# The slot from which VectorE transposes h by way of DRAM: slot 7 in place of slot 12

## The chip, the cores and the metric

The kernel runs on one core of a Trainium2 chip. The time is device time in microseconds of that core, the median of the runs shown; the profile is one more execution, taken by the hardware profiler. TensorE (PE, its weight loads PEld), VectorE (DVE), ScalarE (ACT), GpSimd (POOL) and SyncE (SP) each work through a queue of their own, in order, and wait for one another by semaphores.

## The reference, cut to what matters

Attention with a block-causal mask (8 batches, 8 heads, 576 tokens, 64 wide), then a mixture of experts over its 4608 rows: each row goes to the one expert with the largest logit.

```python
expert_idx = np.argmax(logits, axis=1)
...
for e in range(E):                       # E = 8, D = 512, F = 1024
    mask = expert_idx == e
    ...
    h = np.maximum(x[mask] @ w1[e], 0.0)
    out[mask] = gate_w[mask, None] * (h @ w2[e])
```

All is computed in fp32. For a product the kernel splits each operand into a high part (rounded by a copy to fp32r) and a low part (what is left), and sums three products.

## The kernel before, in words

The first 440 us or so are the attention and the routing. The expert stage after it works in **slots** of 128 rows that belong to one expert; slots 1, 2, 3, ... are written out one after the other, and the order in which the code is written is the order on each engine. The first product of slot g (`layer1(g)`, lines 1046 and 1064) is 24 matmuls of 128x512 on TensorE into two halves `ph`, each turned into half of `h` by a ScalarE relu. The second (`layer2(g)`, lines 1046, 1093 and 1096) is 24 matmuls into `py`, scaled by ScalarE into `y` (`give`) and scattered to the output by GpSimd. `mm3` issues per chunk of 128 channels three matmuls: high part by high weight, high part by low weight, low part by high weight.

**Turning h.** The second product needs h with its channels on the partitions. Two ways are in the kernel.
- By TensorE (`ht`, line 1077): eight 128x128 transposes into `px`, then a ScalarE copy to `hh` and a VectorE subtraction to `hl` (lines 1085 and 1086).
- By VectorE: ScalarE's queue stores each half of h to DRAM as soon as its relu is done (`h_store`, line 1003); GpSimd's queue loads it back in another arrangement into `hq` (`h_load`, four DMAs, line 1011); VectorE transposes blocks of 32x32 into `px`, two instructions (`h_turn`, line 981); then the copy to `hh` and the subtraction to `hl`, each in two halves (`h_in`, lines 990 and 988).

There is one `hq`, one `hh` and one `hl`; `ph` and `px` have three buffers, `py` two. x is turned by VectorE in the same way from slot 7 on in both kernels (`x_turn`, then `xh` on ScalarE and `xl` on VectorE), gathered by GpSimd four slots ahead.

**Weights.** `raw[0]` and `raw[1]` hold the next expert's weights of the first and the second product in fp32. At the first slot of an expert they are split into the other half of `ring_h` (ScalarE, line 808) and `ring_l` (VectorE, line 812), in four pieces of 128x1024, two at a time, and SP then loads the expert after it into raw. At other slots the split is branched over.

What sets the order are the calls in `first` and `second`, which follow one another for each slot (`TURN` is 12, `LAG` is 10):

```python
def seconds(g):
    return g - 1 if g < LAG + 2 else g - 2
def first(g):
    ...
    if g <= LAG + 1:
        ht(g - 1)
    if g != LAG + 2:
        next_weights(seconds(g), 1, (0, 1))
    if g > 1:
        next_weights(g, 0, (2, 3))
    layer1(g, out=g < NU - 1)            # stores h where g >= TURN
def second(g):
    ...
    if g >= XTURN - 1 and g + 2 < NSLOT: # x_turn(g + 2), x_in, x_low
    ...
    if g != LAG + 2:
        next_weights(seconds(g), 1, (2, 3))
    ...
    next_weights(g + 1, 0, (0, 1))
    if g > TURN:
        h_turn(g - 1)
    if g >= TURN:
        h_load(g)
    if g <= LAG:
        layer2(g - 1)
    elif g > LAG + 1:
        layer2(g - 2, y=slots[g + 2]["xg"] if g + 2 < NSLOT else None)
    if LAG + 1 < g <= TURN:
        ht(g - 1)
    ...
    if g + AHEAD < NSLOT:
        fetch(g + AHEAD)
    if g > TURN:
        h_in(g - 1)
```

So with TURN at 12, slots 0 to 11 are turned by TensorE and slots from 12 on by VectorE; `second(11)` has no second product, and from `second(12)` on the second product runs two slots behind the first in place of one.

Of the kernel before, what the change touches and what calls it, by code (L numbers as in the profile page):

```python
# [34 lines left out]
def kernel(  # L35
# [879 lines left out]
        nc.vector.tensor_scalar(tab[:, 3, gs], eg[:, 0], float(E), None, op0=ALU.is_lt)  # L915

    AHEAD = 4
    TURN = 12
    LAG = TURN - 2
    XTURN = 6  # L920
    NFIRST = 4
# [21 lines left out]
    def next_weights(g, i, cs=range(NPC)):  # L943
        if g >= NSLOT:
            return
        sl = slots[g]
        if g == 0:
            for c in cs:
                split_hi(i, c, 1)
                split_lo(i, c, 1)  # L950
            load_raw(i, 2, cs)
            return
        body = sl["body", i]
        for en, fn in (("act", split_hi), ("dve", split_lo)):
            with tc.If(sl["to", en] != 0):  # L955
                to = sl["to", en] & 1
                for c in cs:
                    ins = fn(i, c, to)
                    for en2, c2, o in body:
                        if en2 != en and c2 != c:  # L960
                            tc.declare_no_dep(ins.ins, o.ins, reason="other columns of the ring")
                    body.append((en, c, ins))
        with tc.If(sl["first_sp"] != 0):
            load_raw(i, sl["en2"], cs)

    def fetch(g):
        slots[g]["xg"] = xg = take("xg")
        slots[g]["gate"] = take("gate")
        w = DM // GQ
        parts_of = [(xg, xbuf, rowi[:, g:g + 1])] if g <= XTURN else [  # L970
            (xg[:, j * w:(j + 1) * w], xunit, rowq[:, j, g:g + 1]) for j in range(GQ)]
        for to, src, at in parts_of + [(slots[g]["gate"], gbuf, rowi[:, g:g + 1])]:
            nc.gpsimd.indirect_dma_start(out=to, out_offset=None, in_=src,  # L973
                                         in_offset=bass.IndirectOffsetOnAxis(ap=at, axis=0))
# [27 lines left out]
    def h_store(g, f):  # L1002
        nc.scalar.dma_start(hrows[g % 2][f // 512], slots[g]["h"][:, f:f + 512])

    def h_load(g):

        slots[g]["hq"] = hq = take("hq")
        w = DF // GQ
        for q_ in range(GQ):
            rows = hrows[g % 2][q_ // 2]  # L1010
            nc.gpsimd.dma_start(hq[32 * q_:32 * q_ + 32].rearrange("j (g x) -> j g x", g=GQ),
                                rows[:, q_ % 2 * w:(q_ % 2 + 1) * w].rearrange("(g j) x -> j g x", g=GQ))

    def h_turn(g):
        slots[g]["ht"] = [turned(slots[g]["hq"], slice(f, f + 4), NF) for f in range(0, NF, 4)]

    def h_in(g, us=(0, 1)):
        if 0 in us:
            slots[g]["hT"] = take("hh"), take("hl")
        hh, hl = slots[g]["hT"]  # L1020
        for u in us:
            for w in range(2):
                part(w, hh[:, 4 * u:4 * u + 4], hl[:, 4 * u:4 * u + 4], slots[g]["ht"][u])
# [32 lines left out]
    def layer1(g, out=True):  # L1056
# [4 lines left out]
        for f in range(0, DF, 512):  # L1061
# [3 lines left out]
            slots[g]["h"] = h  # L1065
            if out and g >= TURN:
                h_store(g, f)

    def ht(g, fs=(0, 4), pts=None):
        for f in fs:  # L1070
            ht_copy(g, f, ht_pe(g, f, None if pts is None else pts[f // 4]))
# [28 lines left out]
    def layer2(g, cs=None, y=None):  # L1100
        if cs is None or 0 in cs:
            slots[g]["py"] = take("py")
        py = slots[g]["py"]
        mm3(g, 1, py, slots[g]["hT"], DM, NF, 0, cs)
        if cs is None or NF - 1 in cs:
            give(g, py, slots[g]["gate"][:, 0:1], outi[:, g:g + 1], y)
# [202 lines left out]
    def second(g):  # L1309
# [14 lines left out]
# [11 lines that stand above are left out]
# [5 lines left out]
# [4 lines that stand above are left out]
# [81 lines left out]
```

## Time and profile before

| | |
|---|---|
| median of three runs (lowest, highest) | 864.79 us (864.24, 872.6) |
| the profiled execution | 868.43 us, its span 866.7 us |
| PE busy in the span | 837.9 us (97%) |
| DVE, ACT, POOL busy | 581.5, 488.0, 595.3 us |
| mean granted clock of TensorE | 0.984 |
| bytes moved by DMA | 146.67 MB |

Busy time is time in which the engine had an instruction in work; idle time of an engine is laid to what released it. A granted clock of 1.00 is 2.4 GHz, one of 0.50 is 1.2 GHz.

### The profile page before, as it was taken

Reading aid. Unit: us, or ns where it says so; the run is one execution under the profiler, and the core shown is the slowest. Engines: PE = TensorE matmul, PEld = TensorE weight load, DVE = VectorE, ACT = ScalarE, POOL = GpSimd, SP = SyncE. Lnnn points to the kernel's source line nnn. Section 1 sums busy time; section 2 is a strip of 40 time slices with the busy share of each in tenths; the row PEclk is TensorE's granted clock in tenths of the full one; section 3 lists DMA queues with packets and bytes.
Section 4 is the critical chain, followed back from the end, with each engine's and each line's share of the span. In section 5 each row is a group of like instructions: output and inputs, shape, how many; then the busy total and the mean of one; then the engine's idle time right before and its main releaser. Section 6 shows DMA issues by size and latency. Waiting matters only on the chain. (4 is left out here: it accounts for less than half of the span.)

```text
span 866.7 us, 19006 instructions
## 1 busy us (share of the span) xinstructions
PE 837.9 (97%) x5148; PEld 677.5 (78%) x5148; DVE 581.5 (67%) x1275; ACT 488.0 (56%) x959; POOL 595.3 (69%) x756
## 2 busy tenths in 40 slices
PE   7989999999999999988899999999999999999996
PEld 4768887788877788856678888888888888888875
DVE  8648788888787888882976545745666544666441
ACT  4647776768686767765655534644645333553321
POOL 6555778788788787875644355556777877677872
PEclk9889999999999999998999999999999999999999
DMA  7967878888887889864538444556777554455441
GB/s 149 197 127 149 178 174 177 181 173 180 177 180 169 165 186 184 190 163 151 182 111 292 139 136 147 190 191 211 238 246 239 158 152 148 133 150 148 153 119 38
DMA packets 141531, 146.67 MB, mean 169 GB/s; under 512 B 98889, under 2 KB 108329, under 8 KB 139852
## 3 DMA queue, kind: packets, MB, share of 16 engines
q1 hardware_dynamic: 115868, 91.58, 44.0%
q0 software_dynamic: 18896, 41.45, 17.2%
q10 hardware_dynamic: 6624, 12.06, 3.9%
q8 instruction: 50, 0.82, 0.4%
q14 instruction: 93, 0.76, 0.3%
HBM read 85.12 MB, written 31.79 MB: 135 GB/s over the span
## 5 line engine op out<-in xcount | busy, mean ns | idle before, releaser
L367 DVE TENSOR_REDUCE nmx<-psm 128x1 f32<-128x320 f32 x315 | 134.7, 453 | 65.0 <-PE psm L365 60.4
L410 ACT ACTIVATE pT<-pss 128x448 f32<-128x448 f32 (+1 forms) x254 | 108.5, 449 | 51.6 <-PE pss L401 40.5
L391 POOL TENSOR_TENSOR pS<-pS,pT 128x320 f32<-128x320 f32 x189 | 112.4, 594 | 21.0 <-ACT pT L419 4.4
L401 PE MATMUL pss<-qx,kx 70*128 70x448 f32 (+1 forms) x382 | 109.4, 312 | 10.9 <-DMA qx<-nmT 10.9
L400 PE MATMUL pss<-qb,ka 128*128 128x448 f32 (+1 forms) x382 | 115.1, 313 | 0.3
L1046 PE MATMUL py<-ring_h,hh 128*128 (+1 forms) x288 | 112.7, 391 | 0.8 <-ACT h L1064 0.8
L1046 PE MATMUL py<-ring_h,hl 128*128 (+1 forms) x288 | 112.2, 390 | 0.0
L1046 PE MATMUL py<-ring_l,hh 128*128 (+1 forms) x288 | 112.1, 389 | 0.0
L391 POOL TENSOR_TENSOR pS<-pT 128x448 f32<-128x448 f32 x63 | 71.9, 1141 | 58.1 <-ACT pT L410 57.9
L1046 PE MATMUL ph<-ring_h,xh 128*128 x280 | 109.9, 393 | 0.0
L1046 PE MATMUL ph<-ring_h,xl 128*128 x280 | 109.3, 390 | 0.0
L1046 PE MATMUL ph<-ring_l,xh 128*128 x280 | 109.2, 390 | 0.0
L365 PE MATMUL psm<-kd,qd 128*128 128x320 f32 x315 | 106.2, 373 | 1.9 <-DVE idx L300 0.8
L435 PE MATMUL psb<-pT,vo 128*64 128x448 f32 (+4 forms) x768 | 96.5, 399 | 2.0 <-issue 1.0
L812 DVE TENSOR_TENSOR ring_l<-raw,ring_h 128x1024 f32 (+1 forms) x64 | 83.0, 1308 | 18.7 <-ACT ring_h L808 13.8
L1064 ACT ACTIVATE h<-ph 128x512 f32<-128x512 f32 x70 | 41.8, 598 | 79.4 <-PE ph L1046 68.0
L435 PEld LDWEIGHTS psb<-pT,vo 128*64 128x64 f32 x768 | 50.4, 138 | 45.1 <-issue 29.9
L401 PEld LDWEIGHTS pss<-qx,kx 70*128 70x128 f32 x382 | 73.8, 193 | 13.7 <-DMA qx<-nmT 7.3
L400 PEld LDWEIGHTS pss<-qb,ka 128*128 128x128 f32 x382 | 73.8, 193 | 7.4 <-ACT pT L410 3.4
L973 POOL DMA_INDIRECT xg<-xbuf,rowq x64 | 64.9, 1014 | 21.1 <-issue 18.6
L973 POOL DMA_INDIRECT ex<-xbuf,rowq x64 | 64.1, 1002 | 19.5 <-issue 15.8
L808 ACT CAST ring_h<-raw 128x1024 f32 (+1 forms) x68 | 70.3, 1053 | 6.5 <-ACTq L955 4.1
(278 smaller groups left out, 1812.3 us busy)
## 6 DMA issues: line engine op xcount, KB each, us to landing
raw<-in_moe_w_dram SPq DMA_DIRECT2D x40, 512.0 KB
ka<-kd SPq DMA_DIRECT2D x128, 144.0 KB
raw<-in_moe_w_dram SPq DMA_DIRECT2D x12, 1024.0 KB
hrows<-h ACTq DMA_DIRECT2D x46, 256.0 KB
hq<-hrows POOLq DMA_DIRECT2D x92, 128.0 KB
qn<-in_q_dram SPq DMA_DIRECT2D x64, 144.0 KB
kn<-in_k_dram SPq DMA_DIRECT2D x64, 144.0 KB
qx<-qb SPq DMA_DIRECT2D x32, 288.0 KB
```

What stands on the lines that cost most here:

```text
L365: nc.tensor.matmul(mx[:, 0:max(e - a, 256)], qd[d][:, j, :, :], kd[d][:, a:a + max(e - a, 256)], start=True, stop=True)
L367: nc.vector.tensor_reduce(m[:, j + u:j + u + 1], mx[:, 0:e - a], axis=AX.X, op=ALU.max, negate=True)
L391: eng.tensor_tensor(o, pT[0:r, P:S] if t == 1 else o, pT[0:r, off[t]:off[t] + w], op=ALU.add)
L400: nc.tensor.matmul(o, ka[i][:, hh, ts], qb[i][:, hh, c0:c1], start=True, stop=False)
L401: nc.tensor.matmul(o, kx[i][0:KX, hh, ts], qx[i][0:KX, hh, c0:c1], start=False, stop=True)
L410: nc.scalar.activation(pT[:, o:o + c1 - c0], st[:, 0:c1 - c0], AF.Exp, scale=scale)
L435: nc.tensor.matmul(ob[hh * D:(hh + 1) * D, c0:c1], a[:, t, hh, :], pTs[hh][0][:, o:o + c1 - c0], start=(t == 0), stop=(c0 == OB or t == NJ ...
L808: return nc.scalar.copy(piece(ring_h, to, c, half), raw[i][:, c * CW:(c + 1) * CW])
L812: return eng.tensor_tensor(piece(ring_l, to, c, half), raw[i][:, c * CW:(c + 1) * CW], piece(ring_h, to, c, half).bitcast(F32), op=ALU.sub ...
L973: nc.gpsimd.indirect_dma_start(out=to, out_offset=None, in_=src, in_offset=bass.IndirectOffsetOnAxis(ap=at, axis=0))
L1046: m = nc.tensor.matmul(out, a[:, c, :], w, start=(c == 0 and w is wh and a is sh), stop=(c == nk - 1 and a is sl_))
L1064: nc.scalar.activation(h[:, f:f + 512], ph, AF.Relu)
```

## The change

The number TURN goes from 12 to 7, and LAG with it from 10 to 5. Slots 7 to 11 are now turned by VectorE by way of DRAM; TensorE turns slots 0 to 6. `second(6)` has no second product (it was `second(11)`), and the two slots' distance begins in `second(7)`.

```diff
     AHEAD = 4
-    TURN = 12
+    TURN = 7
     LAG = TURN - 2
     XTURN = 6
     NFIRST = 4
```

TensorE, at the border of slots 7 and 8. Before, the last matmul of the second product of slot 6 is followed by the eight transposes of h of slot 7 (`h_6276`), then comes the first product of slot 8:

```order
L1046 MATMUL py_6682<-ring_h_6494,hl_6279 128x512
L1077 MATMUL px_6680<-ident,h_6276 128x128 x4
L1077 MATMUL px_6678<-ident,h_6276 128x128 x4
L1057 TENSOR_LOAD tab
L1057 ISA x2
L1046 ISA
L1046 MATMUL ph_6675<-ring_h_6207,xh_6218 128x512
```

Now, a slot later (after the second product of slot 6 comes the first product of slot 9), the transposes are gone:

```order
L1046 MATMUL py_6682<-ring_h_6494,hl_6279 128x512
L1057 TENSOR_LOAD tab
L1057 ISA x2
L1046 ISA
L1046 MATMUL ph_6677<-ring_h_6207,xh_6217 128x512
```

From there on TensorE has products alone in its queue.

VectorE, at the head of `first(9)` before. The load of the next slot's flags is followed by the two halves of `hl` of slot 8, which take what TensorE transposed (`px`); the branch, the register and the address rows behind them open the split of the next pieces of weights:

```order
L963 UNCONDITIONAL_BRANCH
L939 TENSOR_LOAD tab
L939 ISA x2
L955 UNCONDITIONAL_BRANCH x2
L1086 TENSOR_TENSOR hl_6279<-px_6680,hh_6278 128x512
L1086 TENSOR_TENSOR hl_6279<-px_6678,hh_6278 128x512
L955 COMPARE_AND_BRANCH
L812 REGISTER_ALU
L812 ISA
```

Now h of slot 8 has its rows at the end of `second(9)`, behind all pieces of the split (the last of them is the first row here): two transposes from `hq`, and `hl` behind them:

```order
L812 TENSOR_TENSOR ring_l_6208<-raw_132,ring_h_6207 128x1024
L955 UNCONDITIONAL_BRANCH x2
L963 UNCONDITIONAL_BRANCH
L981 STREAM_TRANSPOSE px_6678<-hq_6277 128x512
L981 STREAM_TRANSPOSE px_6679<-hq_6277 128x512
L988 TENSOR_TENSOR hl_6279<-px_6678,hh_6278 128x512
L988 TENSOR_TENSOR hl_6279<-px_6679,hh_6278 128x512
```

Two VectorE instructions are added for each of the slots 7 to 11, and `hl` moves from the head of a slot's work to its end. ScalarE gains two store issues, GpSimd's queue four load issues a slot.

## Rows read from the trace of the kernel before

**Rows 1.** Waits of TensorE from 458 us on: waiting line, releaser: total, times, longest

```profile
PE py L1046 <- ACT h L1064: 0.8, 1, 0.8
```

**Rows 2.** Stretches: from:to, length, busy time by engine, granted clock, DMA share, GB/s

```profile
519.18:531.00 11.82, 11.82 (x58) 9.90 (x56) 5.53 (x6) 5.50 (x8) 5.77 (x6) 1.00 0.16 49
612.80:623.68 10.88, 10.88 (x50) 9.01 (x49) 8.48 (x9) 5.65 (x8) 6.32 (x8) 1.00 0.82 279
```

**Rows 3.** Timeline of TensorE: start, length, line, out<-in, count; slots 6 and 15

```profile
519.18 1.05 PE L1077 MATMUL px<-ident,h 128*128 128x128 f32 x8
519.99 0.47 PE L1046 MATMUL ph<-ring_h,xh 128*128 x1
...
623.67 0.39 PE L1046 MATMUL py<-ring_h,hh 128*128 x1
```

**Rows 4.** Timeline of ScalarE from 526 to 592 us: the splits of weights

```profile
527.32 2.13 ACT L808 CAST ring_h<-raw 128x1024 f32 x2 [0.49 <-ACTq L955]
533.57 2.14 ACT L808 CAST ring_h<-raw 128x1024 f32 x2 [0.57 <-ACTq L955]
...
550.42 4.18 ACT L808 CAST ring_h<-raw 128x1024 f32 x4
...
586.41 4.41 ACT L808 CAST ring_h<-raw 128x1024 f32 x4 [0.49 <-ACTq L955]
```

**Rows 5.** Timeline of VectorE in slot 14, in brackets the idle time before

```profile
608.75 1.29 DVE L988 TENSOR_TENSOR hl<-px,hh 128x512 fp32r<-128x512 f32 x2 [1.49 <-ACT hh L990]
611.03 2.55 DVE L812 TENSOR_TENSOR ring_l<-raw,ring_h 128x1024 f32 x2 [0.99 <-ACT ring_h L808]
613.92 1.09 DVE L981 STREAM_TRANSPOSE px<-xg 128x512 f32<-128x512 f32 x1 [0.34 <-DVEq L955]
615.67 0.69 DVE L988 TENSOR_TENSOR xl<-px,xh 128x512 fp32r<-128x512 f32 x1 [0.66 <-PE py L1046]
616.68 2.56 DVE L812 TENSOR_TENSOR ring_l<-raw,ring_h 128x1024 f32 x2 [0.32 <-ACT ring_h L808]
619.57 2.20 DVE L981 STREAM_TRANSPOSE px<-hq 128x512 f32<-128x512 f32 x2 [0.34 <-DMA ex<-xbuf,rowq]
621.68 1.43 DVE L988 TENSOR_TENSOR hl<-px,hh 128x512 fp32r<-128x512 f32 x2
```

**Rows 6.** Timeline of ScalarE in slot 15

```profile
623.89 0.60 ACT L1064 ACTIVATE h<-ph 128x512 f32<-128x512 f32 x1 [0.41 <-PE ph L1046]
...
625.06 0.59 ACT L990 CAST xh<-px 128x512 fp32r<-128x512 f32 x1 [0.57 <-DVE px L981]
626.07 2.14 ACT L808 CAST ring_h<-raw 128x1024 f32 x2 [0.42 <-ACTq L955]
```

**Rows 7.** Timeline of VectorE in slots 8 and 15

```profile
551.56 5.00 DVE L812 TENSOR_TENSOR ring_l<-raw,ring_h 128x1024 f32 x4 [0.32 <-ACT ring_h L808]
...
627.15 2.54 DVE L812 TENSOR_TENSOR ring_l<-raw,ring_h 128x1024 f32 x2 [0.78 <-ACT ring_h L808]
629.61 2.21 DVE L981 STREAM_TRANSPOSE px<-hq 128x512 f32<-128x512 f32 x2
```

**Rows 8.** Timeline of VectorE, two neighbouring turns of h

```profile
663.08 2.20 DVE L981 STREAM_TRANSPOSE px<-hq 128x512 f32<-128x512 f32 x2 [0.34 <-DVEq L955]
...
672.65 2.22 DVE L981 STREAM_TRANSPOSE px<-hq 128x512 f32<-128x512 f32 x2 [1.29 <-DMA hq<-hrows]
```

**Rows 9.** Timeline of GpSimd between those two: the loads of h

```profile
665.57 2.29 POOL L1011 DMA_DIRECT2D hq<-hrows  x4 [0.76 <-DVE px L981]
```

**Rows 10.** Timeline of TensorE: two waits, in the attention and in the routing

```profile
50.24 0.58 PE L401 MATMUL pss<-qx,kx 70*128 70x288 f32 x1 [2.56 <-DMA qx<-nmT]
...
431.59 0.18 PE L558 MATMUL psm<-ohb,triS 128*128 128x40 bf16 x1 [1.61 <-DVE ohb L550]
```

**Rows 11.** Stretches: the clock granted behind those two waits

```profile
50.22:57.04 6.82, 6.80 (x29) 6.69 (x30) 2.56 (x4) 4.31 (x8) 1.99 (x2) 0.50 0.81 137
...
429.09:432.50 3.41, 1.80 (x17) 1.49 (x16) 3.07 (x12) 2.31 (x10) 0.00 (x0) 1.00 0.49 159
```

## The prediction

> **What bounds the kernel now.** I read the waits of TensorE first. From 458 us to the end it waits once, for 0.8 us, in the last slots [rows 1]: the expert stage is TensorE's queue and nothing else, and an instruction taken out of it is time won as long as no other engine becomes late. Next the stretches: a slot whose h TensorE turns takes 11.82 us, one whose h VectorE turns 10.88, both with TensorE busy throughout at full clock [rows 2]. So a product takes 10.88 / 2 = 5.44 us, one matmul 10.88 / 48 = 0.227, and eight transposes cost 11.82 - 10.88 = 0.94. The third reading is of the other engines in a slot of the new kind, since they will now do this work earlier. VectorE works strictly in order: in slot 14, where the second product's weights are split, the transposes of h stand behind both pairs of pieces and begin at 619.57 [rows 5]. The second product that needs them begins at 623.67 [rows 3].
>
> That slot has spare time, and how much decides this case. `hl` comes in two halves; both take 1.43 us from 621.68 [rows 5], and a half takes 0.69 by the equal subtraction of x in the same rows, so the first half is ready at 622.37, 2.80 us after the transposes began. The product's first two matmuls need `hh` alone, so it could start 0.45 before that half is ready. TensorE would have waited only if the turn had come 623.67 + 0.45 - 622.37 = 1.75 us later.
>
> **What the change takes away.** Slots 7 to 11 lose eight transposes each: 5 x 0.94 = 4.7 us of TensorE's queue, all of it on the path. Without any wait that is the gain.
>
> **What it adds on the other engines.** Per slot VectorE gains two transposes (2.20) and loses nothing, ScalarE gains two issues of a store, GpSimd four of a load (2.29 in all [rows 9]). They lie beside 10.88 us of TensorE, of which a slot of the new kind fills 8.48 on VectorE, 5.65 on ScalarE and 6.32 on GpSimd [rows 2], so in sum they are hidden; what can come out is their order. GpSimd's gathers, queued behind the loads, are four slots ahead. About 1 MB of DMA a slot is added. The first products of slots 6 and 7 now follow each other without a second product between; slots 11 and 12 did so before, with four pieces of weights between on ScalarE at 586.41 [rows 4], and TensorE didn't wait [rows 1]. I cost these at nothing.
>
> **Where order matters.** The splits stand at the first slot of an expert. The transposes at 519.18 open `first(6)` [rows 3], so the pair at 527.32 is `second(6)` and that at 533.57 `first(7)`: an expert begins at slot 7. In the same way the four pieces at 550.42 are in `second(8)` (two of the second product of slot 7, two of the first of slot 9), and the four at 586.41 are the first product's at slot 12 [rows 4]. So experts begin at slots 7, 9 and 12, after two and three slots. With the second product two slots behind, the pieces collide in front of a turn: `first(9)` gets four (second product of 7, first of 9), and `second(11)` four (second product of 9, first of 12). No slot of the new kind had four before its turn so far. Four pieces take VectorE 5.00 us [rows 7], a pair 2.55: 2.45 more, against 1.75 spare.
>
> **First wait, h of slot 8.** TensorE's times without waits, from 519.99 [rows 3] by 5.44 a product and 0.94 for slot 6's transposes: first product of slot 7 at 525.43, second of 5 at 530.87, transposes 536.31, first of 8 at 537.25, second of 6 at 542.69, first of 9 at 548.13, second of 8 at 564.45. ScalarE's relu of slot 8 starts 0.22 after 542.69, as 623.89 does after 623.67; its split 2.18 later [rows 6]: 545.1. VectorE's part begins 1.08 later and the turn of slot 7 2.46 after that [rows 7]: 548.6; `hl` is done after 3.54 [rows 5]: 552.2. Then four pieces, 0.99 after `hl` as at 611.03 [rows 5]: 553.2 to 558.2. From the first pair's end in slot 14 (613.58) to the turn are 5.99 us (x, the second pair): slot 8's turn begins at 564.2, its first half is ready at 567.0, and the product starts at 566.5, 2.1 late. Two things in these rows may be shorter here: ScalarE's 0.57 for a late x [rows 6], and some of the 0.99. Lower end 1.3, upper 2.1; I take **1.7**.
>
> **Second wait, h of slot 10.** The second product of slot 8 now starts at 566.15, that of slot 10 two slots later at 587.91. The single `hq` ties the turn of slot 9 to that of 8: the load may only be issued when the turn has read `hq`. Two such turns are 9.57 apart [rows 8], the second held by the landing (loads issued until 667.86 [rows 9], turn at 672.65: 4.8 us). With slot 8's turn at 563.8, slot 9's is at 573.4 by that row; with no wait for the landing VectorE's own rows (3.54 to the end of `hl`, then 3.1 for x with its gaps [rows 5]) give 570.5. Then `hl` 3.54, 0.99, a pair 2.55, and slot 14's 5.99 with 2.45 more, less 0.4 since a turn directly behind the first product's pieces starts without a gap [rows 7]: slot 10's turn at 588.5 or 585.6, and the product can start 2.35 later at 590.9 or 588.0: a wait of 3.0 or 0.1. The row with the landing is the nearer one, since new weights were being loaded there as here; I take **2.3**, below it because the load of those weights may come a little earlier here.
>
> A page of the Trainium skill, "SBUF — State Buffer", section on the DMA setup-cost knee, gives a DMA about 2 us plus its bytes at 436 GB/s, an estimate of 2.3 us for one 128 KB load of h. The 4.8 us above don't agree; by the page the turn of slot 9 would not wait, the second wait would be 0.1, and the sum -4.7 + 1.7 + 0.1 = -2.9, or 861.9 us.
>
> After that, VectorE has one pair in `first(12)` and none until slot 14, where the work stands as before; I see no third wait.
>
> **Sum.** -4.7 + 1.7 + 2.3 = -0.7 us. The profiled execution took 868.43 us, 1.7 of them around its span of 866.7, and 3.6 more than the median of 864.79; I carry the difference over to the median: **864.1 us**.
>
> **Rivals.**
> 1. Nothing waits: the lower ends are still too high, because VectorE follows ScalarE more closely than in slot 14. For it speaks that no slot of the new kind has waited yet [rows 1]; against it, 2.45 more in front of 1.75 spare, twice. 864.79 - 4.7 = 860.1.
> 2. Slower than before: the clock. A wait of 2.56 us for a DMA was followed by 6.82 us at a granted clock of 0.50, one of 1.61 us by none [rows 10, 11]. Half clock for 6.82 us loses 3.4 us of products. My second wait (up to 3.0, in two parts with two matmuls between) is about as long as the wait that was followed by the fall, the first shorter. [...] One fall: 864.1 + 3.4 = 867.5; two: 870.9.
> 3. The added DMA makes the loads of h later still: stretches with weights and h already have a DMA share of 0.82 [rows 2]. Each us of landing beyond 4.8 lengthens the second wait by one, and past 10.88 between turns every slot waits. Two us more at slots 9 and 10 give about 868.
>
> **Chances.** The two short waits (forecast) 0.60, own range 861.5 (1.3 and 0.1) to 865.2 (2.1 and 3.0); nothing waits 0.12; clock falls 0.20, of which twice 0.03; late loads 0.08. From 861.0 to 868.2 leaves out the first rival and the double fall with the worst loads: 8 in 10. A measurement of this kernel can tell some 1%, 8.6 us, from no change: every case but the worst lies within, so faster 0.01, same 0.96, slower 0.03.
>
> **What the profile after would show.** Right: 56 transposes of h in place of 96 at line 1077; slots 9 to 12 at 10.88 us but for two; waits of TensorE at the second products of slots 8 and 10, for ScalarE's `hh` and VectorE's `hl`, 1 to 3 us each; in front of them four pieces at line 812 in a row, in `first(9)` and `second(11)`; VectorE waiting for `hq` before slot 9's turn. Wrong: no such wait, and a time near 860; a stretch at clock 0.50 within 560 to 600 us, and one near 868; waits at other slots, or at a first product for x or weights, which I have at nothing.

## The result, and the profile after

The changed kernel takes **872.17 us** (median of 20 runs, 867.59 to 876.85) where the kernel before, run beside it, takes **866.68 us** (20 runs, 862.28 to 872.6): ratio **1.0058**, 95% interval 1.0039 to 1.0076, some 5 us slower. The forecast was 864.1 us, 0.7 less than the 864.79 us of three runs from which it started; over 20 runs that kernel's median is 1.9 us higher, and the changed kernel lies 8.1 above the forecast. The profiled execution of the changed kernel took 872.16 us, its span 870.3.

The expert stage first. The waits of TensorE in it and behind it are now these (line, releaser: total, times, longest), where the kernel before had one [rows 1]. The row for `h` is that one; the others are new:

```profile
PE py L1046 <- ACT hh L990: 4.0, 2, 2.6
PE py L1046 <- ACT h L1064: 0.9, 1, 0.9
PE py L1046 <- DVE hl L988: 0.6, 3, 0.2
```

TensorE's timeline (start, length, operation, in brackets the gap ahead of it and what ended it) puts the two long ones at the second products of slots 8 and 10:

```profile
562.31 0.39 PE L1046 MATMUL ph<-ring_h,xl 128*128 x1
564.06 0.50 PE L1046 MATMUL py<-ring_h,hh 128*128 x1 [1.36 <-ACT hh L990]
564.40 0.39 PE L1046 MATMUL py<-ring_l,hh 128*128 x1
565.00 0.50 PE L1046 MATMUL py<-ring_h,hl 128*128 x1 [0.21 <-DVE hl L988]
...
589.21 0.50 PE L1046 MATMUL py<-ring_h,hh 128*128 x1 [2.61 <-ACT hh L990]
```

VectorE's timeline ahead of them shows what was forecast: four pieces of weights in front of the turn of h of slot 8 (551.67) and of slot 10 (582.52), and the turn of slot 9 held up by the landing of its load (572.51), the counterpart of [rows 8]:

```profile
551.67 5.03 DVE L812 TENSOR_TENSOR ring_l<-raw,ring_h 128x1024 f32 x4 [0.79 <-ACT ring_h L808]
...
562.26 2.11 DVE L981 STREAM_TRANSPOSE px<-hq 128x512 f32<-128x512 f32 x2 [0.34 <-DVEq L955]
...
572.51 2.21 DVE L981 STREAM_TRANSPOSE px<-hq 128x512 f32<-128x512 f32 x2 [3.52 <-DMA hq<-hrows]
...
582.52 5.00 DVE L812 TENSOR_TENSOR ring_l<-raw,ring_h 128x1024 f32 x4 [0.32 <-ACT ring_h L808]
587.44 2.09 DVE L981 STREAM_TRANSPOSE px<-hq 128x512 f32<-128x512 f32 x2
```

Now three stretches of each kernel: the expert stage from the start of slot 6's first product to the end of the last first product, the last second products, and what is left after the last matmul (from:to, length, busy time of PE, PEld, DVE, ACT and POOL with the number of instructions, granted clock, DMA share, GB/s). The kernel before:

```profile
519.99:841.43 321.44, 321.44 (x1443) 266.53 (x1441) 185.87 (x200) 142.30 (x215) 230.65 (x267) 1.00 0.56 176
841.43:859.75 18.32, 17.54 (x81) 14.37 (x80) 5.05 (x6) 4.10 (x7) 6.08 (x7) 1.00 0.13 36
859.75:866.70 6.95, 0.00 (x0) 0.00 (x0) 0.00 (x0) 0.69 (x1) 1.05 (x2) 0.70 0.17 60
```

The changed kernel:

```profile
517.95:841.15 323.20, 318.64 (x1403) 261.44 (x1401) 196.35 (x210) 144.08 (x215) 243.87 (x287) 1.00 0.62 191
841.15:859.60 18.45, 17.55 (x81) 14.37 (x80) 5.06 (x6) 4.10 (x7) 4.85 (x6) 1.00 0.13 34
859.60:870.30 10.70, 0.00 (x0) 0.00 (x0) 0.00 (x0) 0.69 (x1) 1.97 (x2) 0.72 0.11 38
```

Two things come out. The expert stage has 40 instructions less on TensorE, slots without a wait take 10.88 us as in [rows 2], and yet the stage is 323.20 - 321.44 = **1.8 us longer**; so what was lost there is 1.8 + 4.7 = 6.5 us. And what comes after the last matmul is 10.70 - 6.95 = **3.75 us longer**, in a part that the prediction didn't look at. Together 5.5, as much as the medians differ (872.17 - 866.68 = 5.49). In these two profiles the spans differ by only 3.6, because the attention and routing ended 2.0 us earlier in the one of after (517.95 against 519.99); that part is not touched by the change.

The program ends with a function `last`. GpSimd has a `drain` in it at line 1352, between the scatter of the last slot but two and those of the last two (each `layer2` that is complete issues one scatter; `...` marks what is left out here):

```python
def last(g):
    ...
    layer2(g - 2, range(5, NF))
    h_in(g - 1, (1,))
    nc.gpsimd.drain()
    layer2(g - 1, range(0, 5))
    ...
    layer2(g - 1, range(5, NF))
    ...
    layer2(g, y=slots[g]["xg"])
```

The view of that one line (count, shortest/median/longest in ns, start) in the kernel before, and then in the changed one:

```profile
L1352 POOLq DRAIN  x1: 8130/8130/8130, 849.6 to 849.6; - x1
```

```profile
L1352 POOLq DRAIN  x1: 9750/9750/9750, 849.5 to 849.5; - x1
```

GpSimd's timeline shows the last two scatters of the kernel before, and then the three around the drain in the changed one:

```profile
858.82 1.00 POOL L1096 DMA_INDIRECT out_dram<-y,outi  x1 [7.92 <-DMA out_dram<-xg,outi]
862.54 0.98 POOL L1096 DMA_INDIRECT out_dram<-xg,outi  x1 [2.71 <-POOLq L1365]
```

```profile
849.73 1.01 POOL L1096 DMA_INDIRECT out_dram<-y,outi  x1 [3.52 <-ACT y L1093]
860.30 0.99 POOL L1096 DMA_INDIRECT out_dram<-y,outi  x1 [9.55 <-DMA out_dram<-xg,outi]
865.87 0.98 POOL L1096 DMA_INDIRECT out_dram<-xg,outi  x1 [4.58 <-POOLq L1365]
```

The second stands behind the drain: it goes out 0.70 us after the end of the last matmul (860.30 - 859.60), in the kernel before 0.92 us ahead of it (858.82 - 859.75). That is the 1.62 us by which the drain is longer. The third goes out once the second has landed: 5.57 us after it here, 3.72 before. In the trace's DMA records 60 of the second scatter's 64 data packets land by 862.68 and four between 864.0 and 864.6; a 16 KB packet of the queue that loads instructions was under way from 861.92 to 863.58. In the kernel before all 64 had landed by 861.26, ahead of that packet (861.72). So the third is 1.85 later still. The two delays, 1.62 and 1.85, make up nearly all of the 3.75.

### The profile page after: what moved, and what is told of

It reads as the page before. It is cut to its first block, busy times and chain, and to the rows that moved or that the text cites. A ratio compares the mean times of both kernels' runs of the same rounds, so it can differ in the third digit from the quotient of the medians.

```text
span 870.3 us, 18987 instructions
## 1 busy us (share of the span) xinstructions
PE 834.3 (96%) x5108; PEld 671.4 (77%) x5108; DVE 592.1 (68%) x1285; ACT 489.5 (56%) x959; POOL 608.2 (70%) x776
## 5 line engine op out<-in xcount | busy, mean ns | idle before, releaser
L981 DVE STREAM_TRANSPOSE px<-hq 128x512 f32<-128x512 f32 x56 | 61.5, 1144 | 30.2 <-DMA hq<-hrows 22.0
L1011 POOL DMA_DIRECT2D hq<-hrows x112 | 64.1, 590 | 24.1 <-DVE px L981 17.2
```

The source lines that it names most:

```text
L981: nc.vector.transpose(out.rearrange("p (g c j) -> p g c j", g=GQ, j=32), rows.rearrange("p (g i c) -> p g c i", g=GQ, c=nk)[:, :, cs, :])
```

## Experiments on the end of GpSimd's queue

All times are medians of runs beside the kernel before on the same chip. The first pair and e9 to e18 fell on chips where the kernel before takes 866 to 868 us, e1 to e4 on one where it takes 914.1, e5 to e8 on one where it takes 909.0; there the attention is longer, and the kernel before itself has waits in the expert stage (in e5 1.3 us at one second product, and 2.6 more ahead of slot 13's first product). A stage is compared with one of the same kind of chip only. "Stage" is the length of the first stretch above, "end" that of the third.

| run | ratio (95% interval) | stage, us | drain, us | end, us |
|---|---|---|---|---|
| before, first profile | | 321.44 | 8.13 | 6.95 |
| after, first profile | 1.0058 (1.0039 to 1.0076) | 323.20 | 9.75 | 10.70 |
| e1 the change again | 1.0076 (1.0040 to 1.0113) | 332.52 | 9.75 | 9.64 |
| e2 pieces last | 1.0146 (1.0105 to 1.0187) | 339.81 | 9.75 | 10.34 |
| e3 lag only | 1.0011 (0.9983 to 1.0038) | 328.15 | 8.12 | 6.75 |
| e4 loads only | 1.0001 (0.9975 to 1.0027) | 327.47 | 9.75 | 10.40 |
| e5 before again | 1.0010 (0.9973 to 1.0047) | 326.68 | 8.12 | 7.05 |
| e6 no VectorE pieces | 1.0067 (1.0024 to 1.0110) | 325.31 | 9.75 | 10.66 |
| e7 drain first | 1.0037 (0.9999 to 1.0074) | 332.73 | 9.79 | 5.99 |
| e8 no drain | 1.0095 (1.0057 to 1.0133) | 325.99 | none | 13.01 |
| e9 no pieces | 1.0055 (1.0029 to 1.0081) | 324.65 | 9.75 | 10.49 |
| e10 loads only again | 1.0079 (1.0051 to 1.0107) | 322.75 | 9.75 | 10.12 |
| e11 tail, changed kernel | 1.0049 (1.0021 to 1.0078) | 324.07 | 9.38 | 8.34 |
| e12 tail, kernel before | 0.9984 (0.9964 to 1.0004) | 321.45 | 8.17 | 6.93 |
| e13 small DMAs | 1.0041 (1.0011 to 1.0071) | 321.45 | 9.75 | 10.00 |
| e14 loads by SyncE | 1.0034 (1.0008 to 1.0059) | 326.20 | 8.13 | 6.80 |
| e15 change, SyncE's loads | 1.0075 (1.0042 to 1.0108) | 331.10 | 8.13 | 6.96 |
| e16 fewer DMAs | 1.0001 (0.9976 to 1.0026) | 321.45 | 3.55 | 5.78 |
| e17 change, short drain | 1.0021 (0.9996 to 1.0046) | 324.23 | 4.31 | 6.46 |
| e18 the change again | 1.0062 (1.0036 to 1.0088) | 324.68 | 9.75 | 10.43 |

**e1, e18: the changed kernel again; e5: the kernel before again.** No edit.

> The changed kernel, unchanged, a second time. In its profile the expert stage, from the start of the first product of slot 6 to the end of the last first product, was 323.20 us against 321.44 before, +1.8: the two predicted waits with what follows them cost 6.4, the missing transposes gave back 4.7. What comes after the last matmul's end was 10.7 us against 7.0, +3.7. Theory A (the waits are the loss, the end of the program differs by chance from run to run): the expert stage is again 1.8 longer, the stretch after the last matmul is somewhere between 7 and 11, and over many runs the kernel is about 2 us slower, ratio 1.002. Theory B (the 20 added loads on GpSimd shift something at the end of its queue): the stretch after the last matmul is again over 10 us and the ratio again about 1.006.

> The kernel before, unchanged, so that a profile of it stands beside the others of this group, and as a measure of how far two timings of one kernel differ: ratio 1.000, interval about 0.003 to either side. If the end of GpSimd's queue hangs on the number of its DMAs, the drain in the last slots takes 8.1 us as in both profiles without added loads so far (9.75 us in the four with them), and the stretch after the last matmul is about 7 us.

The end is no chance: 9.64 to 10.70 us behind a drain of 9.75 each time, and 7.05 behind one of 8.12 in the kernel before. e1 is the one profile with the long drain in which the third scatter follows the second at 4.02 us, and the one in which no packet of the instruction queue is under way while the second's data land. In the eight others (the first profile, e2, e4, e6, e9, e10, e13, e18) there is one, the last four data packets land 1.3 us or more behind the rest, and the third scatter follows at 4.94 to 5.57.

**e4 and e10: the loads alone.** The kernel before with

```diff
-            if out and g >= TURN:
+            if out and g >= 7:
                 h_store(g, f)
...
-        if g >= TURN:
+        if g >= 7:
             h_load(g)
```

> The kernel before, whose ScalarE and GpSimd also store and load the rows of h of slots 7 to 11 (the loads are read by nobody; TensorE turns h there as before). So it has the added 5 MB of DMA and the 20 added loads in GpSimd's queue and nothing else of the change. Theory A: 866.7 us, within 1, no new wait of TensorE. Theory B (the number of GpSimd's DMAs moves the end of its queue): 3 us more, about 869.7, with over 10 us after the last matmul. Theory C (DMA traffic makes weights or x late): new waits of TensorE between 530 and 600 us, 868 or more.

> The kernel before with the added stores and loads alone, a second time. Its profile showed 3.4 us more after the last matmul (drain 9.75 in place of 8.12), its times no difference (interval to +2.5 us). Theory B (the end costs 3.4 us in every run): ratio 1.003 to 1.005, drain 9.75. Rival (the longer end is made up for elsewhere, or doesn't count in most runs): ratio 0.998 to 1.001 again.

In both profiles the drain is 9.75 and the end over 10 us though nothing is turned earlier. The times don't agree with each other: no loss in e4, 6.9 us in e10. The end alone is 3.2 to 3.5 us by the profiles, and the stage of e10 is 1.3 longer than in the first profile of the kernel before. Why e4, on the chip of 914 us, shows none of it in its median, and why e10 loses some 2.4 us more than the two together, is not settled.

**e13: small DMAs.** The kernel before with 20 DMAs of a small table in slots 7 to 11, four a slot.

```diff
+        if 7 <= g <= 11:
+            for q_ in range(GQ):
+                nc.gpsimd.dma_start(rowa[32 * q_:32 * q_ + 32], rowsd.rearrange("(g j) s -> j g s", g=GQ))
```

> The kernel before with 20 more DMAs issued by GpSimd in slots 7 to 11, of some hundred bytes a partition, into a table that nobody reads any more: no added traffic to speak of. Theory B (the number of GpSimd's DMAs sets the length of its drain): drain 9.75 us in place of 8.12, 10 to 10.7 us after the last matmul in place of 7, expert stage as before, ratio 1.003 to 1.005. Rival (the bytes do it): drain 8.12, 7 us after the last matmul, ratio 1.000.

As theory B says. The stage is that of the kernel before to 0.01 us, and the end is the changed kernel's:

```profile
521.64:843.09 321.45, 321.44 (x1443) 266.52 (x1441) 185.79 (x200) 142.51 (x215) 245.27 (x287) 1.00 0.57 177
...
861.00:871.00 10.00, 0.00 (x0) 0.00 (x0) 0.00 (x0) 0.69 (x1) 1.99 (x2) 0.63 0.12 42
```

The line of its drain:

```profile
L1355 POOLq DRAIN  x1: 9752/9752/9752, 850.9 to 850.9; - x1
```

So 20 more DMAs in GpSimd's queue, issued 260 us or more ahead of the drain, cost 3 us by the profile and 3.5 by the medians (870.29 against 866.74; the interval of the ratio is some 1 to 6 us), though they move next to nothing.

**e14: the same bytes, loads issued by SyncE; e16: fewer GpSimd DMAs in the kernel before; e17: the change with fewer.**

```diff
+        eng = nc.sync if g >= 17 else nc.gpsimd
         for q_ in range(GQ):
             rows = hrows[g % 2][q_ // 2]
-            nc.gpsimd.dma_start(hq[32 * q_:32 * q_ + 32].rearrange("j (g x) -> j g x", g=GQ),
+            eng.dma_start(hq[32 * q_:32 * q_ + 32].rearrange("j (g x) -> j g x", g=GQ),
```

This is e16 on the kernel before and e17 on the changed one; e14 is the kernel of e4 with `g < 12` as the condition.

> The kernel before with the added stores and loads of h of slots 7 to 11 (read by nobody), the added loads issued by SyncE in place of GpSimd: the same bytes, no more GpSimd DMAs. Theory B: drain 8.12, 7 us after the last matmul, and what is left is at most the 1.3 us that the expert stage grew in the run with GpSimd's loads: ratio 1.000 to 1.002. Rival (the bytes do it): drain 9.75, ratio 1.004 to 1.008.

> The kernel before with the loads of h from slot 17 on issued by SyncE, some 40 GpSimd DMAs fewer. Theory B: the drain falls to about 5 us (0.08 us for each DMA), the scatter of the last slot but one goes out as soon as its product is written, and the stretch after the last matmul falls from 7 to about 5.5 us: ratio 0.998, where no load of h becomes late. Rival (the drain depends on something else): drain 8.1, ratio 1.000.

e14 has the bytes, and its drain is as short as before:

```profile
L1353 POOLq DRAIN  x1: 8130/8130/8130, 856.3 to 856.3; - x1
```

With e13 that leaves the count. Its stage is 4.8 us longer all the same, in waits of 0.5 to 0.8 us for weights and for h; with these loads in it SyncE's queue probably makes other things late, which no run shows by itself. e16 has 72 DMAs fewer ahead of the drain and a drain of 3.55. Its end is 1.2 us shorter (the forecast was 1.5), and its ratio shows nothing of it: in its profile the stretch ahead of the end is 1.0 us longer (855.22 - 835.94 = 19.28 against 18.32), by a wait that is laid to no engine. Where this drain is shorter, the program's last one is longer: 2.81 us in e16 and 3.68 in e17, against 2.2 behind drains of 8.13 and 9.75 at the same place. So the price of a DMA isn't constant: with 369 issued before it begins the drain takes 3.55 us, with 389 (e17) 4.31, with 441 8.13, with 461 9.75; from 0.04 us each to 0.08.

> The changed kernel with the loads of h from slot 17 on issued by SyncE (as in the run with fewer DMAs, where no load became late), those of slots 7 to 16 by GpSimd as in the change. Theory: drain about 5.2 us (3.55 and 1.62 for the 20 loads), some 5.8 us after the last matmul, so 4.5 us less than the changed kernel's end and 1.2 less than the end before; the expert stage is longer than before by the 1.8 to 2.6 us of the changed kernel's profiles, since the waits (6 to 7 us) are more than the transposes (4.7). Ratio 1.000 to 1.002. If the waits were only as long as predicted (4.0 us together), the stage would be 0.7 shorter than before and the ratio 0.997 to 0.998.

> The changed kernel again, on the chip of the run beside it: drain 9.75, 10 us or more after the last matmul, waits at the second products of slots 8 and 10, ratio 1.006 to 1.007, and some 4 to 5 us above the run beside it.

e17 against e18 on one chip: ends of 6.46 and 10.43 us, medians of 869.84 and 872.52, stages alike. The end is 2.7 us of the loss by the medians, 4.0 by the profiles; the intervals of the two ratios overlap, so that this pair alone would not show it, and e13 does. What is left, ratio 1.0021, is the stage, 2.8 us longer than in the first profile of the kernel before, a little more than was expected of e17; its interval still takes in no loss.

**e7, e8, e11, e12: the drain moved or left out.** e7 puts the drain first in `last`, e8 drops it, e11 and e12 (the same on the kernel before) add to e7

```diff
-        layer2(g - 1, range(5, NF))
+        layer2(g - 1, range(5, NF), y=slots[g - 1]["xg"])
```

> The changed kernel with GpSimd's drain at the beginning of the last slots, where its queue is idle, in place of after the scatter of the last slot but two. Theory B (the drain, 1.6 us longer with the 20 added loads, holds up the last two scatters): the drain still takes about 9.75 us, but ends some 3 us ahead of the last matmul's end; the stretch after the last matmul falls from 10.7 to 7 or 8 us and the kernel is 3 us faster than the changed one, ratio 1.002 to 1.004 against before. Rival (the last scatters wait for something else, for each other's landing above all): the stretch stays at 10 us or more, ratio 1.006 to 1.008.

> The changed kernel without that drain. If the drain is work that has to be done once in any case, the last drain of the program grows from 2.2 us to 10 or more and the stretch after the last matmul from 10.7 to 14 or more, ratio 1.010; if it is only a wait for the scatters under way, the scatter of the last slot but one goes out 5 us ahead of the last matmul's end, and the stretch falls to 6 or 7 us, ratio 1.001 to 1.002.

> The changed kernel with the drain at the beginning of the last slots and the second product of the last slot but one written to a free buffer of x rather than to the only y, for which ScalarE waited (3.6 us of TensorE) when the drain alone was moved. Theory B: 5.5 to 6.5 us after the last matmul, no wait of TensorE behind the last first product but the one of 0.9; 4 us faster than the changed kernel, ratio 1.001 to 1.003 against before. Rival: the scatters still follow each other only after landing, so that 8 us or more remain after the last matmul.

> The kernel before with the same two edits in the last slots. Its drain is 8.1 us and ends 1.6 us earlier against the last matmul, so less is to be won: 5.5 to 6 us after the last matmul in place of 7, ratio 0.998 to 0.999. If the gain of the same edits in the changed kernel is about as small (1 us), the longer drain is not what the changed kernel's end suffers from.

e7 shortened the end to 5.99 us but gave it back ahead of it. In its profile (an execution of 926.07 us, the median is 915.24) the stretch from the last first product to the last matmul is 24.05 us in place of 18.45, most of that at a new wait. The scatter of the last slot but two now went out late, ScalarE waited 7.4 us for the only `y`, and TensorE for ScalarE's next copy:

```profile
913.34 0.50 PE L1046 MATMUL py<-ring_h,hh 128*128 x1 [3.61 <-ACT hh L1085]
```

e8: most of the drain's time goes into the last one of the program, 8.65 us in place of 2.2, and the end grows to 13.0. e11 has no such wait and an end of 8.34, less good than forecast: with the drain ahead of all three, the last scatters follow each other at 3.6 to 3.7 us, each after the landing of the one ahead. e12 gained nothing at its end (6.93), its last scatters 3.5 to 3.6 us apart, and its ratio says no more.

## Experiments on the waits

**e2: weight pieces behind the turn.** `next_weights` of `second(g)` moved behind `h_in(g - 1)` from slot 8 on.

> The changed kernel with the weight pieces of second(g) issued after the turn and the split of h instead of ahead of them, from slot 8 on, so that at an expert's border VectorE and ScalarE have at most two pieces less ahead of the turn. Theory A (pieces ahead of the turn make both waits): the waits at the second products of slots 8 and 10 shrink to under 0.5 us together, the expert stage falls by 4 to 6 us against the changed kernel, the whole to 862 to 863 us where the kernel before has 866.7, ratio 0.995 to 0.996. Theory B (the end of GpSimd's queue): the expert stage gains the same, but the stretch after the last matmul stays over 10 us: 865.5 to 866.5, ratio 0.999. Theory C (the added 1 MB of DMA a slot is what makes h late): the waits stay at 1 us or more each, about 870.

The worst of all, and as none of the three theories had it: slot 10's wait is gone, slot 8's is not. Its list of waits in the expert stage has first products that wait for weights three times, 2.2 us in all, where e1 on the same chip has one of 0.8:

```profile
PE py L1046 <- ACTq L955: 3.8, 2, 2.0
PE py L1046 <- DVEq L955: 3.4, 5, 1.1
PE py L1046 <- issue: 3.2, 4, 1.1
PE ph L1046 <- DVE ring_l L812: 2.2, 3, 1.0
```

**e3: the lag alone.** The kernel before with `LAG = 5`.

> The kernel before with the second product two slots behind from slot 6 on, but VectorE's turn from slot 12 on as it was, so that TensorE turns h of slots 7 to 11 in the new order and nothing is stored or loaded for them. Theory A: no gain (the 40 transposes stay) and no wait over 0.5 us in the expert stage, since TensorE's own transposes need no room in VectorE's queue; 866.7 us, within 1. Theory B: the same, stretch after the last matmul about 7. If the new order of products is itself the loss (weights of an expert's second product one slot later, the four pieces together): waits of 1 to 3 us at slots 8 to 11, 868 to 870.

By its time the order of the products costs nothing that can be measured. Its profile has a stretch all the same that was not expected: from the second product of slot 5 to the first of slot 8 it is 3.7 us longer than in e4, on the same chip and in the old order. TensorE stands there and then has a granted clock of 0.50 for 3.4 us, while VectorE waits for weights that land late:

```profile
573.15 1.23 DVE L812 TENSOR_TENSOR ring_l<-raw,ring_h 128x1024 f32 x1 [4.73 <-DMA raw<-in_moe_w_dram]
```

The changed kernel has such a stretch on the chips of 909 and 914 us too (1.3 to 3.6 us more in e1, e2, e6, e7 and e8) and on none of the others, so it is no part of the 1.8 us of the first profiles.

**e6 and e9: pieces left out,** VectorE's two pairs in e6, both engines' in e9:

```diff
         for en, fn in (("act", split_hi), ("dve", split_lo)):
+            if en == "dve" and (g, i, tuple(cs)) in ((7, 1, (0, 1)), (9, 1, (2, 3))):
+                continue
```

e9 has this without the test of `en`.

> The changed kernel, in which VectorE leaves out two pairs of its weight pieces: the pair of the second product of slot 7 in first(9) and that of slot 9 in second(11), so that no slot has four pieces ahead of a turn of h (the low halves of these weights are then old ones, so the values of some tokens are not the reference's). Theory A (four pieces ahead of the turn make the waits): the second products of slots 8 and 10 wait for under 0.3 us each, the expert stage from the start of the first product of slot 6 to the end of the last first product falls from 323.2 to some 317.5 us on a chip like that of the first profiles. With the end as in the changed kernel (10.7 us after the last matmul) this gives 866.0 where before has 866.7, ratio 0.999. Rival (the load of h through DRAM lands too late, whatever VectorE does): the wait of slot 8 goes and that of slot 10 stays over 1.5 us, ratio 1.002 to 1.003.

> As the run without VectorE's two pairs, but ScalarE leaves its share of the same pieces out as well (both halves of these weights are then old ones; they are still loaded). Theory A' (the four pieces make the waits, by way of ScalarE, whose four pieces end before VectorE's can, and whose relu, stores and copies stand behind them): now the second products of slots 8 and 10 wait under 0.4 us each, and the time is 866.7 - 4.7 + 3.4 for the end = about 865.5 on a chip like the first, ratio 0.998 to 1.001. Rival (the load of h lands too late): the product of slot 10 waits 1.5 us or more still; the landing to the turn of slot 9 is then the last thing ahead of it, ratio 1.003.

In e6 both waits stayed (1.58 and 2.51 us; 1.69 and 1.54 in e8 on the same chip, 1.76 and 3.14 in e1 on the one of 914 us). VectorE merely waited for ScalarE, which still had four pieces to make: first ScalarE's row, then VectorE's, from the two timelines.

```profile
588.23 4.16 ACT L808 CAST ring_h<-raw 128x1024 f32 x4 [0.39 <-issue]
```

```profile
591.34 2.54 DVE L812 TENSOR_TENSOR ring_l<-raw,ring_h 128x1024 f32 x2 [2.78 <-ACT ring_h L808]
```

In e9, with ScalarE's share gone too, slot 8 no longer waits and slot 10 waits 0.60 in place of 2.6. So the four pieces make the two waits. But the stage is no shorter, 324.65 us. TensorE, now 3.2 us earlier (slot 15's first product starts 95.9 us after slot 6's, in the changed kernel 99.1), finds h of slots 13 and 14 not ready; here slots 10 and 13:

```profile
583.04 0.50 PE L1049 MATMUL py<-ring_h,hh 128*128 x1 [0.60 <-ACT hh L993]
619.73 0.50 PE L1049 MATMUL py<-ring_h,hh 128*128 x1 [2.29 <-ACT hh L993]
```

The turn of slot 13 waits for loads that GpSimd had issued by 610.88, 7 us earlier (the turn on VectorE, then the loads on GpSimd):

```profile
617.95 2.10 DVE L984 STREAM_TRANSPOSE px<-hq 128x512 f32<-128x512 f32 x2 [2.05 <-DMA hq<-hrows]
```

```profile
608.59 2.29 POOL L1014 DMA_DIRECT2D hq<-hrows  x4
```

**e15: the change, its added loads issued by SyncE.**

The condition `g < 12` of e14 on the changed kernel.

> The changed kernel with the 20 added loads (slots 7 to 11) issued by SyncE. Theory B together with the waits (A): drain 8.12, 7 us after the last matmul, the expert stage still 1 to 3 us longer than before because waits of 6 to 8 us in all stand against the 4.7 us gained; ratio 1.001 to 1.004. If SyncE's queue, in which the loads stand behind those of the weights, makes h later than GpSimd's did: more waits, ratio 1.006 or more. If the waits go: below 0.998.

With SyncE's loads h came later: five waits for `hh`, 7.6 us in all, and a stage of 331.10 with a short drain. It tells nothing of the waits in the changed kernel; e17 does.

## Why the prediction was wrong

**The mechanism of the two waits was right.** They stand at the slots named, behind the pieces named, with the load of slot 9 between. The gain is 4.7 as costed, and the added turns fit beside TensorE in sum.

**The term that failed is the added loads, "I cost these at nothing".** I followed them into the slots where they are issued, and not to the end of the queue they are issued in. They lengthen a drain 260 us or more later, by 1.62 us, and the last two scatters go out later by that and by what the second then takes to land. e13 shows it without the change, e14 shows the same bytes without it. The price is 3.0 to 3.75 us by profiles of chips like the first, 3.5 by the medians of e13.

**The two waits were mis-sized, 1.7 and 2.3.** By the distance between the starts of neighbouring products beyond 5.44 us, slot 8's product cost 2.14 (1.52 ahead of it, 0.62 inside) and slot 10's 3.40 (2.77 and 0.63). In e11, e17 and e18 the two together cost 5.2, 6.5 and 7.0. Ahead of the first matmul the two are 4.29 in the first profile, where I had 4.0. What was missed is the 0.62 inside each: I counted to the moment at which the first matmul can start, and the third, the first that needs `hl`, then starts 0.94 us behind it (565.00 - 564.06) in place of 0.45. Part of the second wait is the landing of slot 9's load. The turns of slots 8 and 9 are 10.25 apart (572.51 - 562.26) where the row gave 9.57, so it came 0.7 later than by the row. That the turn was forecast for 573.4 and came at 572.51 is no sign for the row, since the stage began 2.0 us earlier in this profile. I also put VectorE's queue in front, with ScalarE's four pieces hidden beside it; e6 shows ScalarE to be the one that leads. The times came out near all the same, probably because the waits for ScalarE are in VectorE's rows. The estimate by the page "SBUF — State Buffer" of the Trainium skill (section on the DMA setup-cost knee), which had no wait there, doesn't agree: VectorE stood 3.52 us.

**"I see no third wait" failed too.** 6.46 - 2.14 - 3.40 = 0.9 us more went in small waits at slots 14, 17 and 18. They are not much in the changed kernel, but e9 shows what stands behind them: the slots with new weights after slot 12 had little to spare, and the 3.2 us that TensorE gained ahead of them in e9 were spent there. The prediction took the work there as before, and didn't ask whether TensorE would come to it earlier.

**The rivals.** "Nothing waits" is out. The clock, with 0.20, did not fall in the first profile of the changed kernel (wait of 2.61 us); it did in e1, e6, e15 and e18 (below). Late loads cost 0.7 us more than the row at slot 9, and are the limit in e9.

**What is left open:** why e4's median shows no loss, why a drain grows with the DMAs ahead of it, and what the four late packets of the last scatter but one wait for. That the packet of the instruction queue holds them up is read from the times of nine profiles, e1 being the one without it; no run was made to move it.

## What to carry to other kernels

A DMA of GpSimd was paid for in three places here: at its issue, at its landing, and at a later point that waits for its queue as a whole. Follow an added instruction to the end of its queue, and read the last 20 us of the profile before costing it at nothing. An engine that is made faster arrives earlier at every later tight place, and e9 lost its gain there; so look for the smallest margin downstream, not only for that of the slots that are changed.

## What the runs showed of the hardware

**GpSimd's drain took the same time in every profile with the same number of DMAs ahead of it, and longer with more:** at its place in `last` 8.12 to 8.13 us in five profiles with 441 of them, 9.75 in nine with 461, on chips whose times differ by 5%; 3.55 with 369 and 4.31 with 389, in one profile each.

**TensorE's clock fell behind waits of h in some runs.** In e18 a wait of 2.55 us was followed by a granted clock of 0.50 (1.2 GHz), and by 1.00 again from 595 us on:

```profile
589.00:592.00 3.00, 2.15 (x6) 1.44 (x7) 2.21 (x3) 1.97 (x3) 1.75 (x4) 0.85 0.94 311
592.00:594.00 2.00, 2.00 (x6) 1.58 (x5) 1.23 (x1) 1.79 (x3) 1.70 (x2) 0.50 1.07 377
594.70:597.00 2.30, 2.30 (x12) 1.88 (x11) 1.65 (x3) 0.72 (x2) 1.69 (x3) 1.00 1.02 274
```

It cost 1.6 us (the product was 2.22 longer than 5.44, 0.62 without a fall), half of the 3.4 that I took from the attention's row. Falls followed waits of 2.51 (e6), 3.14 (e1) and 3.29 us (e15) as well, none the 2.61 of the first profile or the 2.27 of e17. So the length of the wait alone does not tell whether the clock falls.
